# Full attention layers: scores issued in runs of three tiles (a key tile and a half), then the values of the run before, then side matmuls

## The chip, the cores and the metric
The kernel runs on one core of one Trainium2 chip. A core has TensorE (PE in the profile: matmuls; PEld: its weight loads), VectorE (DVE), ScalarE (ACT), GpSimd (POOL) and SyncE (SP), which issues most DMAs. The engines run by themselves and wait for each other through semaphores; each does its own instructions in the order in which they were written. The metric is the device time of one execution in microseconds (us), lower being better.

## The reference
Four attention layers stand one behind the other, on a sequence of 2048 rows of width 512 with 32 heads of 16. Layers 0 and 2 (weights A) see a window of 256 keys, layers 1 and 3 (weights B) all earlier and later keys:

```python
x = A_x
x = x + _A_ref(_layernorm(x, axis=-1), A_wqkv, A_wo)
x = x + _B_ref(_layernorm(x, axis=-1), B_wqkv, B_wo)
x = x + _A_ref(_layernorm(x, axis=-1), A_wqkv, A_wo)
x = x + _B_ref(_layernorm(x, axis=-1), B_wqkv, B_wo)

# _B_ref, after q, k, v = split(x @ wqkv):
scores = jnp.einsum("bhqd,bhkd->bhqk", q, k) * scale
p = _softmax(scores, axis=-1)
o = jnp.einsum("bhqk,bhkd->bhqd", p, v)
return (lambda x, *d: x.transpose(*d))(o, 0, 2, 1, 3).reshape(B, S, D) @ wo
```

## The kernel before
In a full layer the queries are cut into four chunks (`c`) of 512 and the heads into eight head groups (`qd`) of four; layer 3 also goes by quarters (`t`) of two groups each. For a chunk and a head group `attn_full` goes over sixteen key tiles (`j`) of 128 keys. So there are 32 head groups in each full layer, and 512 key tiles.

For a key tile, `exps` is called twice, for two heads each (`pr`). It makes a score tile, 128 keys x 2 heads x 512 queries, with two matmuls of 64 rows each (the two heads lie in different rows of the array and run side by side; q and k are split in high and low halves, and 64 rows hold these parts of a head). Then ScalarE takes the exponential of the whole tile, 128x1024, from PSUM into a tile `e` in SBUF. There are three score tiles in PSUM: two of the pool `ps_s` and one named `third`, taken in turn; a tile is used again when its exponential is done. There are six tiles `e` (`EB`).

The values (`pv`, L821) are four matmuls, one for each head, of 128 keys x 17 columns (16 of V and a column of ones that gives the denominator) by 512 queries in float32, into four strips of the accumulator `acc[0]`, where the sixteen key tiles are summed. They stand in a queue `pvq` and are issued by `flush(2)`: those of a key tile come after the scores of the second key tile behind it. When the last key tile of a head group is through, `epilogue` has VectorE read `acc[0]` (`ot`, L729), and the next group's values wait for that.

Behind the values of each key tile come side matmuls: the projections of q, k and v, and the output matmuls of other chunks and layers, which fill the second accumulator `acc[1]` in groups (L395, each of them in four strips of 32 columns). The class `Side` keeps them in a list. Its `step` is called once for each key tile, and `share` issues as many as a budget allows; the budget rises by the rest of the work over the rest of the steps, or by a least rate. `clock[0]` is the planner's own time, which says when a transfer or a read is expected to be done. TensorE's instructions come in just the order in which this code issues them (`manual_schedule`).

When a group of side matmuls of q or k is through, `project` has VectorE read `acc[1]` twice (L557 and L558: the rounded product, and what is left of it) and GpSimd square the rounded one (L563), for a bound on the scores.

The window layers use the same `exps`, `flush` and `Side`, with three tiles for a head group.

Of the kernel before, what the change touches and what calls it, by code (L numbers as in the profile page):

```python
# [9 lines left out]
F32 = mybir.dt.float32  # L10
# [19 lines left out]
R = 64  # L30
# [4 lines left out]
RUN = 4  # L35
L_MIN = 2.0 ** -90
# [153 lines left out]
def fast_path(ctx, tc, flag, a_x, a_wqkv, a_wo, b_wqkv, b_wo, out):  # L190
# [330 lines left out]
    def project(l, s, c, act, ht=None, first=False):  # L521
# [20 lines left out]
        for t in range(NHT) if ht is None else (ht,):  # L542
# [10 lines left out]
            with tc.high_priority(HEAD_START):  # L553
                if act:
                    nc.scalar.activation(sp[:, 0], ps, AF.Copy, scale=e)
                else:
                    nc.vector.tensor_scalar(sp[:, 0], ps, e, None, op0=ALU.mult)  # L557
                LAST["DVE"] = nc.vector.scalar_tensor_tensor(sp[:, 1], ps, e, sp[:, 0], op0=ALU.mult, op1=ALU.subtract).ins  # L558
            sq = vp.tile([P, QC], BF16, name=f"sq{n}_{t}", tag="sq", bufs=NHT)
            if act:  # L560
# [197 lines left out]

    def exps(name, kt, qt, pr, pieces):

        turn["s"] += 1
        ps = PH["third"] if PH["full"] and turn["s"] % 3 == 0 else ps_s.tile([P, 2, QC], F32, name=f"s{name}", tag="s")
# [6 lines left out]
        spent(0.27)  # L769
        e = pp.tile([P, 2, QC], F32, name=f"e{name}", tag="e", bufs=EB)  # L770
        LAST["ACT"] = nc.scalar.activation(e[:, :, w0:w1], ps[:, :, w0:w1], AF.Exp, scale=SCALE).ins  # L771
        return e

    def flush(n):
        while len(pvq) > n:
            spent(1.0)
# [35 lines left out]

    def attn_full(l, c, qd, kt, qt, a):
        for j in range(NT):
            es_ = []
            for pr in range(2):
                es_.append(exps(f"{l}_{c}_{qd}_{j}_{pr}", kt[j // 8], qt, pr, [(j % 8 * P, 0, QC, 0)]))

            def pv(j=j, es_=es_):
                for h in range(4):  # L820
                    nc.tensor.matmul(a[32 * h:32 * h + DH + 1, :], V[l, qd // 4, j // 8][:, j % 8, 4 * (qd % 4) + h, :],  # L821
                                     es_[h // 2][:, h % 2, :], start=(j == 0), stop=(j == NT - 1),
                                     skip_group_check=True)
            yield pv
# [106 lines left out]
    class Side:  # L931

        def __init__(self, steps, works=(), following=(), least=0.0):
            self.next, self.least = list(following), least
            self.q, self.steps, self.cost, self.spent, self.k = [], steps, 0.0, 0.0, 0
            self.budget = self.lag = 0.0
# [45 lines left out]
        def step(self):  # L982
            self.k += 1
# [16 lines left out]
        def share(self):  # L1000

            self.budget = min(self.budget + max((self.cost - self.spent) / max(self.steps - 3 - self.k, 1), self.least), 0.75)
            self.lag = max(self.lag - max(0.29, self.least), -0.3)
# [325 lines left out]
```

## Time and profile before
| | us |
|---|---|
| median of three runs | 2648.86 |
| lowest and highest run | 2648.67, 2651.83 |
| span of the profiled execution | 2650.4 |
| TensorE busy in it | 2579.3 (97%) |
| ScalarE busy | 2385.8 (90%) |
| VectorE busy | 844.9 (32%) |
| GpSimd busy | 582.9 (22%) |
| exponentials (L771), busy | 2248.1 in 2432 |
| values of the full layers (L821), busy | 1079.7 in 8192 |

No time of its own is kept for the profiled execution beside its span, which lies between the lowest and the highest run. The granted clock of TensorE is 0.996 of full speed in the mean. The full layers run from about 447 to 1400 us and from 1688 to 2635 us, the window layers before each of them.

How to read rows: a row of the order of time has its start, its length, the engine, the line, the operation, output<-input, and the shapes; x8 says that eight such instructions were merged, and the length is then that of them all. What stands in square brackets is the idle time ahead of it and what ended that. A float32 matmul of the values shows as two records, so x8 are the four heads of one key tile. In a row of windows stand the stretch, its length, and for each engine the busy time and the number of instructions.

### The profile page before, as it was taken

To read this page: it belongs to the slowest core of one execution; us is meant where nothing else is said; L and a number is where in the kernel's file an instruction comes from. 1 tells how busy PE (TensorE), PEld (TensorE's weight loads), DVE (VectorE), ACT (ScalarE), POOL (GpSimd) and SP (SyncE) were. 2 spreads that over 40 slices of the span, in tenths; PEclk is the share of its full clock that TensorE was granted. 3 is DMA by queue.
4 is the path that set the end of the run, shared out by engine and by line. 5 is a ranking of instruction groups with operands and counts; after the bars stand their busy time and mean duration, and the time that the engine had idled before them with its cause. 6 is when DMAs were issued, how large, how long until landed. Compare 5 with 4: busy or idle time off the path is not lost.

```text
span 2650.4 us, 63235 instructions
## 1 busy us (share of the span) xinstructions
PE 2579.3 (97%) x26201; PEld 771.5 (29%) x26201; DVE 844.9 (32%) x1947; ACT 2385.8 (90%) x2725; POOL 582.9 (22%) x1215
## 2 busy tenths in 40 slices
PE   8999899999999999999999999999999999999998
PEld 3333344322222222222223444422222222222221
DVE  5746653112332223112216666211111112222121
ACT  5777665999999999999997787699999999999997
POOL 1789760000000000000006788000000000000000
PEclk9999999999999999999999999999999999999999
DMA  6878766223342334222425655423222234435441
GB/s 206 195 229 274 209 197 184 59 97 122 101 108 91 96 114 121 75 76 86 136 69 167 206 159 152 147 77 95 83 77 69 85 106 143 147 113 168 131 134 50
DMA packets 293186, 341.34 MB, mean 129 GB/s; under 512 B 105929, under 2 KB 199593, under 8 KB 288281
## 3 DMA queue, kind: packets, MB, share of 16 engines
q1 hardware_dynamic: 284376, 310.17, 39.2%
q0 software_dynamic: 8512, 27.04, 3.8%
q8 instruction: 207, 3.39, 0.5%
q14 instruction: 91, 0.74, 0.1%
HBM read 226.49 MB, written 96.99 MB: 122 GB/s over the span
## 4 chain that ended last, share of the span: by engine, by line
PE 86%; ACT 6%; DVE 4%; issue 3%; DMA 1%; POOL 1%; SPq 0%; ACTq 0%; DVEq 0%
PE acc L821 34%; PE s L767 23%; PE acc L395 11%; PE b L398 7%; PE acc L855 6%; ACT e L771 5%; PE b L395 3%; PE bs L398 2%; DVE ot L729 1%; DMA x<-in_A_x_dram 0%; DVE xh L471 0%; POOL e L847 0%; PE acc L582 0%; DVE sp L558 0%; POOL e L844 0%
## 5 line engine op out<-in xcount | busy, mean ns | idle before, releaser
L771 ACT ACTIVATE e<-s 128x1024 f32<-128x1024 f32 (+2 forms) x2432 | 2248.1, 1091 | 106.8 <-PE s L767 95.7
L821 PE MATMUL acc<-e,vt 128*17 128x512 f32 x8192 | 1079.7, 599 | 4.3 <-DVE ot L729 3.3
L767 PE MATMUL s<-qt,kt 64*128 64x512 f16 (+3 forms) x5440 | 750.4, 354 | 23.3 <-ACT e L771 10.8
L767 PEld LDWEIGHTS <-kt 64*128 64x128 f16 x5440 | 190.3, 94 | 696.3 <-issue 680.0
L821 PEld LDWEIGHTS acc<-e,vt 128*17 128x17 f32 x8192 | 136.4, 95 | 396.2 <-issue 363.7
L847 POOL TENSOR_SCALAR_AFFINE_SELECT e<-e 128x256 f32<-128x256 f32 x512 | 233.4, 464 | 73.9 <-ACT e L771 72.9
L729 DVE STREAM_TRANSPOSE ot<-acc 128x512 f32<-128x512 f32 x128 | 91.4, 714 | 481.3 <-PE acc L821 375.5
L844 POOL TENSOR_SCALAR_AFFINE_SELECT e<-e 128x256 f32<-128x256 f32 x448 | 195.9, 444 | 42.5 <-ACT e L771 40.5
L855 PE MATMUL acc<-e,vt 128*17 128x384 f32 (+2 forms) x2816 | 197.9, 390 | 0.6 <-POOL e L844 0.5
L398 PE MATMUL b<-xc,w 128*128 128x512 f16 x520 | 125.4, 386 | 8.8 <-DMA xc<-xh 5.6
L671 DVE COPY vt<-acc 128x256 f32<-128x256 f32 (+1 forms) x48 | 23.6, 491 | 336.6 <-PE acc L395 336.6
L395 PE MATMUL acc<-wv,xc 128*32 128x256 f16 (+1 forms) x2304 | 120.6, 299 | 0.2 <-DVE km L598 0.2
L751 POOL TENSOR_TENSOR oh<-o,oh 128x512 f16<-128x512 f32 x19 | 22.1, 1162 | 433.0 <-DVE oh L750 429.7
L395 PEld LDWEIGHTS <-xc 128*32 128x32 f16 x2688 | 77.1, 97 | 137.7 <-issue 133.0
L676 POOL TENSOR_SCALAR vt<-vt 128x16 f32<-128x16 f32 (+1 forms) x48 | 11.1, 232 | 464.8 <-DVE vt L671 464.7
L395 PE MATMUL acc<-xc,w 128*32 128x512 f16 x1344 | 108.0, 379 | 0.0
L563 POOL TENSOR_TENSOR sq<-sp 128x512 bf16<-128x512 f16 x28 | 29.1, 1039 | 349.0 <-DVE sp L557 349.0
L395 PE MATMUL acc<-xc,w_h 128*32 128x512 f16 x1296 | 105.7, 379 | 0.0
L563 POOL TENSOR_TENSOR sq_h<-sp_h 128x512 bf16<-128x512 f16 x27 | 28.1, 1039 | 339.8 <-DVE sp_h L557 278.9
L712 DVE SCALAR_TENSOR_TENSOR x<-acc,x 128x512 f32<-128x512 f32 x60 | 41.4, 690 | 177.1 <-PE acc L395 164.7
L557 DVE TENSOR_SCALAR sp<-acc 128x512 f16<-128x512 f32 x28 | 19.4, 691 | 242.3 <-PE acc L395 242.3
L557 DVE TENSOR_SCALAR sp_h<-acc 128x512 f16<-128x512 f32 x27 | 18.5, 686 | 229.0 <-PE acc L395 229.0
(165 smaller groups left out, 1780.9 us busy)
## 6 DMA issues: line engine op xcount, KB each, us to landing
kt<-kf SPq DMA_DIRECT2D x126, 512.0 KB
xd<-x SPq DMA_DIRECT2D x96, 256.0 KB
qt<-qs SPq DMA_DIRECT2D x96, 256.0 KB
x<-xd SPq DMA_DIRECT2D x96, 256.0 KB
w<-wd SPq DMA_DIRECT2D x16, 1024.0 KB
qs<-sp SPq DMA_DIRECT2D x48, 256.0 KB
wv<-wd SPq DMA_DIRECT2D x20, 512.0 KB
x<-in_A_x_dram SPq DMA_DIRECT2D x32, 256.0 KB
```

The lines of the kernel that those rows point to most:

```text
L395: nc.tensor.matmul(ps[g:g + 32], a[:, g:g + 32], b, start=(i == 0), stop=(i == len(pairs) - 1), skip_group_check=True)
L398: nc.tensor.matmul(ps, a, b, start=(go and i == 0), stop=(i == len(pairs) - 1))
L557: nc.vector.tensor_scalar(sp[:, 0], ps, e, None, op0=ALU.mult)
L563: nc.gpsimd.tensor_tensor(sq, sp[:, 0], sp[:, 0], ALU.mult)
L712: nc.vector.scalar_tensor_tensor(xs[i], ps, 1.0 / (UP[2] * UP[3]), xs[i], op0=ALU.mult, op1=ALU.add)
L729: nc.vector.transpose(ot.rearrange("p b r -> p (b r)"), a)
L767: nc.tensor.matmul(ps[:, h, s0:s0 + wd_], kt[R * h:R * h + R, pr, kc:kc + P], qt[R * h:R * h + R, pr, qc:qc + wd_], start=True, stop=True)
L771: LAST["ACT"] = nc.scalar.activation(e[:, :, w0:w1], ps[:, :, w0:w1], AF.Exp, scale=SCALE).ins
L821: nc.tensor.matmul(a[32 * h:32 * h + DH + 1, :], V[l, qd // 4, j // 8][:, j % 8, 4 * (qd % 4) + h, :], es_[h // 2][:, h % 2, :], start=(j ...
L844: last = nc.gpsimd.affine_select(v, v, pattern=[[0, 2], [-1, P]], compare_op=ALU.is_gt, fill=0.0, base=0, channel_multiplier=1)
L847: last = nc.gpsimd.affine_select(v, v, pattern=[[0, 2], [1, P]], compare_op=ALU.is_ge, fill=0.0, base=0, channel_multiplier=-1)
L855: nc.tensor.matmul(a[32 * h:32 * h + DH + 1, q * P:(q + nb) * P], V[l, (4 * c + j) // 4][:, j % 4, 4 * qd + h, :], es_[h // 2][:, h % 2, s ...
```

## The change
A table `RUNS` cuts the sixteen key tiles of a head group into eleven runs: five times (tile j, first half of tile j+1) and (second half of tile j+1, tile j+2), and last tile 15 alone. "Half" is by queries: `exps_part` puts 256 queries of all four heads into one score tile (four matmuls of 256 columns), so that a key tile and a half are three score tiles and each exponential is still 128x1024. The matmuls of the values of a half are 256 wide and go to the half of the accumulator that they belong to. A run issues its three score tiles one behind the other, then `flush(1)` the values of the run before, and then the side matmuls.

`Side` counts in rooms now: the first run of a head group has room for four side matmuls, the next nine for two each, the last for none (22 for a head group); the budget may exceed a run's room by 1.2 matmuls. The planner's clock goes on by 0.903 for each score tile. In the full layers the square moves from GpSimd to VectorE and stands between its two reads of `acc[1]`.

On TensorE, in layer 1, chunk 2, head group 4, around key tile 7, there stood before (s are score tiles, s1_5721 is `third`, e exponentials, both with layer, chunk, head group, key tile and pair; acc0 and acc1 are the two accumulators; a wait on ScalarE reads Activation, one on VectorE DVE; left out are weight loads, the matmuls that complete a pair, and the other three strips of a side matmul):

```order
L767 MATMUL s1_2_4_7_0_13056<-qt1_2_4_12581,kt1_2_4_0_12583 128x512 [waits Activation_49]
...
L767 MATMUL s1_2_4_7_1_13061<-qt1_2_4_12581,kt1_2_4_0_12583 128x512 [waits Activation_49]
...
L821 MATMUL acc0_81<-e1_2_4_5_0_13020,vt1_1_0_5794 17x512 x2
L821 MATMUL acc0_81<-e1_2_4_5_1_13025,vt1_1_0_5794 17x512 x2
L395 MATMUL acc1_82<-xc2_1_12760,w2_1_1_12702 32x512
...
L767 MATMUL s1_5721<-qt1_2_4_12581,kt1_2_4_1_12585 128x512 [waits Activation_49]
...
L767 MATMUL s1_2_4_8_1_13078<-qt1_2_4_12581,kt1_2_4_1_12585 128x512 [waits Activation_49]
```

and now, with the pieces of a half named p0 and p1 (the rows left out are of the same kinds, and one side matmul of the following three is shown by its first strip):

```order
L786 MATMUL s1_2_4_6_0_13847<-qt1_2_4_13325,kt1_2_4_0_13327 128x512 [waits Activation_49]
...
L786 MATMUL s1_5721<-qt1_2_4_13325,kt1_2_4_0_13327 128x512 [waits Activation_49]
...
L834 MATMUL s1_2_4_7_p0_13856<-qt1_2_4_13325,kt1_2_4_0_13327 128x256 [waits Activation_49]
...
L858 MATMUL acc0_81<-e1_2_4_4_p1_13813,vt1_1_0_5823 17x256 x4
L858 MATMUL acc0_81<-e1_2_4_5_0_13817,vt1_1_0_5823 17x512 x2
L858 MATMUL acc0_81<-e1_2_4_5_1_13822,vt1_1_0_5823 17x512 x2
L399 MATMUL acc1_82<-xc2_1_13583,w2_1_1_13530 32x512 [waits DVE_49]
```

Two score tiles, each waiting for ScalarE, and one key tile of values have become three score tiles, each waiting, and one and a half key tiles of values; the buffers of the three are all that there are, in turn.

On TensorE at the end of layer 1, where the last score tile of head group 7 of chunk 3 is followed by the first of layer 2 (s2), there stood before:

```order
L767 MATMUL s1_3_7_15_1_16976<-qt1_3_7_16309,kt1_3_7_1_16313 128x512 [waits Activation_49]
...
L821 MATMUL acc0_81<-e1_3_7_13_0_16948,vt1_1_1_6659 17x512 x2
L821 MATMUL acc0_81<-e1_3_7_13_1_16952,vt1_1_1_6659 17x512 x2
L821 MATMUL acc0_81<-e1_3_7_14_0_16961,vt1_1_1_6659 17x512 x2
...
L821 MATMUL acc0_81<-e1_3_7_15_0_16974,vt1_1_1_6659 17x512 [waits Activation_49]
...
L821 MATMUL acc0_81<-e1_3_7_15_1_16979,vt1_1_1_6659 17x512 [waits Activation_49]
...
L767 MATMUL s2_0_0_0_0_17018<-qt2_0_0_17011,kt2_0_0_17010 128x384 [waits PE_49]
```

and now:

```order
L786 MATMUL s1_3_7_15_1_18206<-qt1_3_7_17442,kt1_3_7_1_17446 128x512 [waits Activation_49]
...
L858 MATMUL acc0_81<-e1_3_7_13_p1_18168,vt1_1_1_6768 17x256 x4
L858 MATMUL acc0_81<-e1_3_7_14_0_18173,vt1_1_1_6768 17x512 x2
...
L399 MATMUL acc1_82<-wv2_2_0_0_16848,xc2_2_16898 32x512 [waits DVE_49]
...
L858 MATMUL acc0_81<-e1_3_7_15_0_18204,vt1_1_1_6768 17x512 [waits Activation_49]
...
L858 MATMUL acc0_81<-e1_3_7_15_1_18209,vt1_1_1_6768 17x512 [waits Activation_49]
...
L786 MATMUL s2_0_0_0_0_18298<-qt2_0_0_18291,kt2_0_0_18290 128x384 [waits PE_49]
```

Twelve side matmuls (48 with their strips; `wv2_2` are the values' weights of layer 2, chunk 2) now stand between the values of tile 14 and of tile 15. Counted over the program, layer 1 has 748 side matmuls of 512 columns' worth (two of 256 counted as one) and layer 3 651, before and now.

The core of the diff:

```diff
+RUNS = [r for j in range(0, NT - 1, 3) for r in (((j, None), (j + 1, 0)), ((j + 1, 1), (j + 2, None)))] + [((NT - 1, None),)]
+ROOM = [4] + [2] * (len(RUNS) - 2) + [0]
+ROOMS = sum(ROOM)
+LATE = sum(ROOM[:8])
...
+                sq = vp.tile([P, QC], BF16, name=f"sq{n}_{t}", tag="sq", bufs=NHT)
+                if PH["full"]:
+                    nc.vector.tensor_tensor(sq, sp[:, 0], sp[:, 0], ALU.mult)
                 LAST["DVE"] = nc.vector.scalar_tensor_tensor(sp[:, 1], ps, e, sp[:, 0], op0=ALU.mult, op1=ALU.subtract).ins
-            sq = vp.tile([P, QC], BF16, name=f"sq{n}_{t}", tag="sq", bufs=NHT)
-            if act:
+            if PH["full"]:
+                pass
+            elif act:
...
+    def exponentials(name, ps, w0=0, w1=QC):
+
+        spent(0.23 if PH["full"] else 0.27)
+        e = pp.tile([P, 2, QC], F32, name=f"e{name}", tag="e", bufs=EB)
+        LAST["ACT"] = nc.scalar.activation(e[:, :, w0:w1], ps[:, :, w0:w1], AF.Exp, scale=SCALE).ins
+        return e
...
+        ps = score_tile(name)
-            spent(1.0)
+            spent(0.2 if PH["full"] else 1.0)
...
+    def exps_part(name, kt, qt, kc, half):
+
+        ps, w = score_tile(name), QC // 2
+        for pr in range(2):
+            for h in range(2):
+                nc.tensor.matmul(ps[:, h, pr * w:pr * w + w], kt[R * h:R * h + R, pr, kc:kc + P],
+                                 qt[R * h:R * h + R, pr, half * w:half * w + w], start=True, stop=True)
+        return exponentials(name, ps)
+
     def attn_full(l, c, qd, kt, qt, a):
-        for j in range(NT):
-            es_ = []
-            for pr in range(2):
-                es_.append(exps(f"{l}_{c}_{qd}_{j}_{pr}", kt[j // 8], qt, pr, [(j % 8 * P, 0, QC, 0)]))
-
-            def pv(j=j, es_=es_):
-                for h in range(4):
-                    nc.tensor.matmul(a[32 * h:32 * h + DH + 1, :], V[l, qd // 4, j // 8][:, j % 8, 4 * (qd % 4) + h, :],
-                                     es_[h // 2][:, h % 2, :], start=(j == 0), stop=(j == NT - 1),
-                                     skip_group_check=True)
+        for r, run_ in enumerate(RUNS):
+            PH["room"], PH["span"] = ROOM[r], 0.0
+            made = []
+            for j, half in run_:
+                n, k, kc = f"{l}_{c}_{qd}_{j}", kt[j // 8], j % 8 * P
+                if half is None:
+                    made.append((j, half, [exps(f"{n}_{pr}", k, qt, pr, [(kc, 0, QC, 0)]) for pr in range(2)]))
+                else:
+                    made.append((j, half, exps_part(f"{n}_p{half}", k, qt, kc, half)))
+                PH["span"] += 0.903 if half is not None else 1.806
+
+            def pv(made=made):
+                w = QC // 2
+                for j, half, e in made:
+                    for h in range(4):
+                        if half is None:
+                            to, fr = slice(0, QC), e[h // 2][:, h % 2, :]
+                        else:
+                            to, fr = slice(half * w, half * w + w), e[:, h % 2, h // 2 * w:h // 2 * w + w]
+                        nc.tensor.matmul(a[32 * h:32 * h + DH + 1, to], V[l, qd // 4, j // 8][:, j % 8, 4 * (qd % 4) + h, :],
+                                         fr, start=(j == 0), stop=(j == NT - 1), skip_group_check=True)
+                    spent(0.86 if half is None else 0.43)
             yield pv
...
-            self.k += 1
+            self.k += PH["room"] if PH["full"] else 1
...
-            self.budget = min(self.budget + max((self.cost - self.spent) / max(self.steps - 3 - self.k, 1), self.least), 0.75)
-            self.lag = max(self.lag - max(0.29, self.least), -0.3)
-            while self.q and clock[0] >= PH["free"] and self.budget >= MM / 2 and (self.lag < 0.25 or self.budget > 0.45):
+            room = PH["room"]
+            if not room:
+                return
+            self.budget = min(self.budget + room * max((self.cost - self.spent) / max(self.steps - 4 - self.k, 1), self.least), (room + 1.2) * MM)
+            while self.q and clock[0] >= PH["free"] and self.budget >= MM / 2:
                 c = self.one()
                 if c is None:
                     break
                 self.budget -= abs(c)
-                self.lag += abs(c)
...
-                    sd = sd or Side(NT * NQD // 2, works[0], works[1], 0.33)
+                    sd = sd or Side(ROOMS * NQD // 2, works[0], works[1], 0.24)
...
-                        clock[0] = max(clock[0], began + (2.4 if win else 1.8))
+                        clock[0] = max(clock[0], began + (2.4 if win else PH["span"]))
                         began = clock[0]
                         pvq.append([f])
-                        flush(2)
+                        flush(2 if win else 1)
```

The remaining lines replace `NT` by `ROOMS` and the least rates by the same per head group (0.33 x 16 by 0.24 x 22, 0.28 x 16 by 0.204 x 22), and the two points where a work has to be done by then.

22 lines of the change are left out of this document (10 added, 12 removed).

## The prediction
> **What bounds the kernel now.** I read the page first, then the two full layers alone (windows), then the order of time on TensorE and ScalarE inside them. The page says that TensorE is busy nearly all the time and ScalarE not much less, and that the chain that ended last runs 86% over TensorE:
>
> ```profile
> PE 2579.3 (97%) x26201; PEld 771.5 (29%) x26201; DVE 844.9 (32%) x1947; ACT 2385.8 (90%) x2725; POOL 582.9 (22%) x1215
> PE 86%; ACT 6%; DVE 4%; issue 3%; DMA 1%; POOL 1%; SPq 0%; ACTq 0%; DVEq 0%
> L767 PE MATMUL s<-qt,kt 64*128 64x512 f16 (+3 forms) x5440 | 750.4, 354 | 23.3 <-ACT e L771 10.8
> core 0: us, PE busy (x) PEld busy (x) DVE busy (x) ACT busy (x) POOL busy (x), PEclk, DMA share, GB/s
> 447.30:1399.60 952.30, 942.19 (x9408) 225.88 (x9405) 212.01 (x474) 946.93 (x1022) 53.13 (x71) 1.00 0.33 98
> 1688.30:2634.70 946.40, 935.88 (x9137) 234.76 (x9135) 174.73 (x383) 943.12 (x1024) 49.98 (x62) 1.00 0.35 105
> ```
>
> The last two rows are the full layers, 1 and 3, the only stages that the change orders anew. Both engines are 99% busy there, so the shares don't say which one sets the pace; the spacing does. Layer 1 does an exponential in 952.30/1022 = 0.932 us, layer 3 in 946.40/1024 = 0.924, and each layer has 1024, so they take 954 and 946 us, 1900 of the span of 2650.4.
>
> What ScalarE can do at most shows where there is little side work:
>
> ```profile
> 2449.07 1.99 ACT L771 ACTIVATE e<-s 128x1024 f32<-128x1024 f32 x2
> 2449.07 13.91 ACT L771 ACTIVATE e<-s 128x1024 f32<-128x1024 f32 x15
> ```
>
> Two exponentials end at 2451.06, fifteen at 2462.98: 11.92/13 = 0.917 us each. At that pace a layer takes 939 us. So ScalarE's floor for both layers is 1878, and only 22 us (15 and 7) lie between it and now. What lies between is TensorE's work, here in layer 1:
>
> ```profile
> 1041.77 0.40 PE L395 MATMUL acc<-xc,w 128*32 128x512 f16 x4
> 1042.10 0.61 PE L767 MATMUL s<-qt,kt 64*128 64x512 f16 x4
> 1042.64 1.05 PE L821 MATMUL acc<-e,vt 128*17 128x512 f32 x8
> 1043.51 0.61 PE L395 MATMUL acc<-xc,w 128*32 128x512 f16 x8
> 1044.06 0.61 PE L767 MATMUL s<-qt,kt 64*128 64x512 f16 x4
> ...
> 1052.13 1.05 PE L821 MATMUL acc<-e,vt 128*17 128x512 f32 x8
> 1053.11 0.60 PE L767 MATMUL s<-qt,kt 64*128 64x512 f16 x4
> ```
>
> Four score matmuls (two score tiles) take 0.54 us from their start to that of the values, the values 0.87, a side matmul 0.22 (0.33 from 1041.77 to 1042.10 with one, 0.55 from 1043.51 to 1044.06 with two), and 0.11 comes once before the next scores (without any side matmul they start 0.98 after the values). A key tile is 0.54 + 0.98 = 1.52 us plus 0.216 for each side matmul (0.55 less 0.33, in round figures), against 2 x 0.917 = 1.83 on ScalarE. TensorE is the later one with two side matmuls (1.95), ScalarE with one or none.
>
> **The change part by part.** *Fewer bursts.* Sixteen bursts of scores per head group become eleven. Of a burst's 0.54 the two pairs stream 0.43 (each is as wide as a side matmul, 0.216), so 0.11 is the switch to the values, and 0.11 is the switch back. That takes 5 x 0.22 = 1.1 us from TensorE per head group, 70 us over the 64 head groups, but the path can win only the 22 us down to ScalarE's floor. Splitting a key tile by queries should cost nothing by itself. The window layers have 256-wide pieces:
>
> ```profile
> 1435.08 0.63 PE L855 MATMUL acc<-e,vt 128*17 128x256 f32 x8
> 1435.52 1.91 PE L395 MATMUL b<-xc,w 128*32 128x512 f16 x32
> 1437.36 0.39 PE L767 MATMUL s<-qt,kt 64*128 64x256 f16 x4
> 1437.68 1.06 PE L855 MATMUL acc<-e,vt 128*17 128x384 f32 x16
> ```
>
> Two half-wide pairs of scores plus the switch take 0.32 (two full ones 0.54, so 0.11 for a half against 0.22), half-wide values 0.44 (half of 0.87). The pace of an exponential is unchanged, as its form is still 128x1024. Per run TensorE has 0.54 + 0.22 for three score tiles, 1.31 for one and a half tiles of values, 0.11 for the switch, and on average 748/351 = 2.1 side matmuls in layer 1 (counted in the new order) at 0.216: 2.64 us. ScalarE needs 2.75. By work alone TensorE is no longer the later one.
>
> *The wait that is added.* There are three score buffers, and a run fills all three back to back. Its third matmul pair can't start before the third exponential of the run before has ended, and everything on TensorE, values and side matmuls included, stands behind it. What such a wait costs is in the trace of before, where the second pair of a burst waits for the exponential that frees its buffer:
>
> ```profile
> 2450.59 0.92 PE L767 MATMUL s<-qt,kt 64*128 64x512 f16 x4
> 2451.11 0.39 PE L767 MATMUL s<-qt,kt 64*128 64x512 f16 x2
> 2451.44 1.05 PE L821 MATMUL acc<-e,vt 128*17 128x512 f32 x8
> 2449.98 2.00 ACT L771 ACTIVATE e<-s 128x1024 f32<-128x1024 f32 x2
> 2450.88 2.02 ACT L771 ACTIVATE e<-s 128x1024 f32<-128x1024 f32 x2
> 838.65 0.61 PE L767 MATMUL s<-qt,kt 64*128 64x512 f16 x4
> 839.14 1.02 ACT L771 ACTIVATE e<-s 128x1024 f32<-128x1024 f32 x1 [0.58 <-PE s L767]
> ```
>
> The burst at 2450.59 lasts 0.92 and not 0.61 us, because its second pair starts at 2451.11, 0.05 after an exponential ended (2451.06, above), and the values follow 0.33 later. The other two rows are a place where ScalarE had run dry: scores start at 838.65, their exponential at 839.14 and it ends at 840.16, 1.51 us after the scores' start.
>
> The page "TensorE: Matmul & The Clock Gate" of the Trainium skill (Part 3, The mechanism) states that matmuls are strictly first in, first out, without reordering. The trace agrees with that: the values at 2451.44 need nothing of the late pair and still start after it. By this rule the losses below stand; were it not so, the values would pass the late pair and the time would be the first rival's.
>
> So from the third pair of one run to the third pair of the run after next there is a round trip: 0.33 to the values; the values and side matmuls of that run; 0.11 to the next run's first scores; 1.51 to the end of their exponential; two exponentials more, 1.83; 0.05 to the matmul that waits for the last. That is 3.83 us plus values plus side matmuls, and ScalarE alone needs 6 x 0.917 = 5.50 for two runs. The work behind the waiting pair may thus be 1.67 us. Values take 1.31. One side matmul fits (1.52), two are 0.07 over, three 0.29 over, and nothing catches up, because ScalarE has no pace in hand. In the first run of a head group values are one key tile, 0.44 less, so four there count as two.
>
> The new order gives pairs of neighbouring runs by the longer of the two: layer 1 has 18 pairs that fit, 49 at 0.07, 2 at 0.18, 101 at 0.29 and 5 at 0.50, in sum 35 us; layer 3 has 50, 40, 1, 84 and 1, in sum 28. One run's loss covers its neighbour's, since the two round trips overlap; if it did not, the sums would be 51 and 42.
>
> *The end of layer 1.* Twelve side matmuls now stand between the values of tile 14 and those of tile 15 of the last head group: 12 x 0.216 = 2.6 us, with no scores behind them that would feed ScalarE. I count all of it.
>
> *The turn of a head group.* Before, the first values of a group waited for VectorE to read the accumulator:
>
> ```profile
> PEld acc L821 <- DVE ot L729: 16.9, 30, 1.5
> PEld acc L821 <- DVE ot L729: 10.4, 27, 0.7
> ```
>
> (layer 1, then layer 3). This is part of TensorE's lateness, thus of the 22 us, and isn't counted again. Now one run of side matmuls and three score tiles lie in between, more than the read takes.
>
> *The squares.* 55 of them move from GpSimd to VectorE, between the two reads of the side accumulator:
>
> ```profile
> L563 POOL TENSOR_TENSOR sq<-sp 128x512 bf16<-128x512 f16 x28 | 29.1, 1039 | 349.0 <-DVE sp L557 349.0
> L471 DVE TENSOR_TENSOR xh<-xn,xh 128x512 f16<-128x512 f32 x52 | 39.3, 756 | 1.6 <-ACT xh L466 0.4
> L750 DVE CAST oh<-o 128x512 f16<-128x512 f32 x52 | 25.1, 483 | 1.5
> L557 DVE TENSOR_SCALAR sp<-acc 128x512 f16<-128x512 f32 x28 | 19.4, 691 | 242.3 <-PE acc L395 242.3
> ```
>
> On VectorE a square isn't shown; the nearest rows are a cast of one operand (0.48) and an operation with two (0.76). The accumulator comes free that much later. What hides it are the scores and values of the run that follows, 0.76 + 1.31 = 2.07 us, against 0.69 for the first read, up to 0.76 and about 0.69 again for the second, 2.14. I take 0; the excess would be 55 x 0.07 = 4 us, and without the cover it is 55 x 0.76 = 42. GpSimd's 1.04 was off the path, so nothing is won.
>
> **The sum.** 2650.4 (the profiled span, which lies within the runs' 2648.67 to 2651.83) - 22 (down to ScalarE's floor) + 35 + 28 (round trips) + 2.6 = 2694. The median of the runs is 1.5 below that span; I predict 2693.
>
> **The rivals.** *ScalarE alone sets the pace*: the third pair finds its buffer free early enough, and TensorE's 2.64 stay hidden under 2.75. That gives 2650.4 - 22 + 2.6 = 2631, faster. For it speaks the work per run; against it the 0.05 and the 1.51 above. It needs a round trip about 0.3 us shorter than its rows say. The page "TensorEngine Tiling (Array Packing)" of the Trainium skill (Key Properties) says that a change of tiling mode drains the engine; the 0.22 per burst agree with that, and by this rule alone the kernel would come out here.
>
> *The wait and the gain cancel*: a round trip 0.2 us shorter (for instance if a pair's exponential ended 1.3 after it and not 1.51, where ScalarE has no earlier work queued). Two side matmuls then fit, three are 0.09 over: 185 x 0.09 + 6 x 0.3 = 18 us, 2650.4 - 22 + 18 + 2.6 = 2649, no change. Against it: the 1.51 is from just such a place.
>
> *Every long run pays for itself*: losses of neighbouring runs add up, 51 + 42: 2650.4 - 22 + 93 + 2.6 = 2724. It decides if the run that follows a late one can't use the time in which ScalarE stood; late reads of the side accumulator by VectorE would push the same way. That the change doesn't do what it says is excluded by the new order: eleven bursts per head group, as many exponentials.
>
> **How the numbers follow.** Forecast 0.63 (own range 2679 to 2707, from 0.05 us either way on 185 pairs with three side matmuls and 89 with two), ScalarE alone 0.14, cancelled 0.09, every run pays 0.14. The range of 2645 to 2720 leaves out the first rival and the upper half of the last. About 0.2% (5 us) is what a measurement of this kernel can tell from no change: faster 0.14 + 0.02, same 0.06 (the rest of the cancelled case is split), slower 0.78.
>
> **What would show it.** In the profile after: exponentials 0.94 to 0.96 us apart over each full layer; ScalarE idle before about every sixth exponential, ended by the scores; TensorE's scores waiting for ScalarE by tens of us, where the page has 10.8 in all; and the third pair of a run 0.05 after an exponential's end. Wrong would be the forecast if exponentials ran at 0.917 throughout, if the third pair never waited, or if the idle time of TensorE were ended by VectorE and not by ScalarE.

## The result, and the profile after

The changed kernel takes **2691.16 us** (median of four runs, 2687.18 to 2691.7) against 2649.64 (2648.67 to 2651.83) for the kernel before: a ratio of 1.0154, 95% interval 1.014 to 1.0169. The forecast was 2693. The profiled execution of the changed kernel, which the views show, is the shortest of its four runs (2687.18, span 2685.4): the span is 1.8 us shorter than the run's time, and 1.7 to 1.8 in every other run for which both are kept. By the same 1.8 us the profiled execution of the kernel before (span 2650.4) took 2652.2 us, a little over the longest of its runs, 2651.83. So the two spans differ by 35.0 us, and 6.5 of the 41.5 between the medians are not in the traces.

First the page: busy time by engine, the chain that ended last, the costliest groups of ScalarE and of the scores.

```profile
PE 2562.2 (95%) x30041; PEld 982.5 (37%) x30041; DVE 861.0 (32%) x2002; ACT 2401.9 (89%) x2725; POOL 525.8 (20%) x1160
PE 69%; ACT 20%; issue 5%; DVE 3%; DMA 1%; POOL 1%; ACTq 0%; SPq 0%; DVEq 0%
L776 ACT ACTIVATE e<-s 128x1024 f32<-128x1024 f32 (+2 forms) x1792 | 1703.1, 1033 | 112.2 <-PE s L786 95.9
L786 PE MATMUL s<-qt,kt 64*128 64x512 f16 (+3 forms) x4184 | 573.4, 344 | 50.4 <-ACT e_p L776 35.0
L834 PE MATMUL s_p<-qt,kt 64*128 64x256 f16 x1664 | 163.1, 272 | 22.4 <-ACT e L776 20.6
```

TensorE is busy 17 us less than before, though the program is 35 us longer, and part of the chain has moved from TensorE (86% before, 69% now) to ScalarE (6% before, 20% now). That fits a round trip between two engines: neither is busy all the time, and the chain passes from one to the other. The scores wait for ScalarE 35.0 + 20.6 us in these two groups alone, where the page before had 10.8.

The windows from the first exponential of a full layer to the last, both layers (stretch, its length, then busy time and instructions of each engine):

```profile
core 0: us, PE busy (x) PEld busy (x) DVE busy (x) ACT busy (x) POOL busy (x), PEclk, DMA share, GB/s
443.80:1416.70 972.90, 938.30 (x11310) 337.89 (x11311) 218.30 (x501) 956.36 (x1025) 24.14 (x42) 1.00 0.32 96
1704.80:2670.20 965.40, 925.84 (x11061) 333.11 (x11057) 182.35 (x410) 953.22 (x1024) 21.84 (x35) 1.00 0.34 104
```

In the kernel before the same windows read:

```profile
447.30:1402.40 955.10, 944.86 (x9430) 226.63 (x9426) 212.01 (x474) 949.74 (x1024) 53.13 (x71) 1.00 0.33 98
1688.30:2634.80 946.50, 935.98 (x9139) 234.79 (x9137) 174.73 (x383) 943.23 (x1024) 49.98 (x62) 1.00 0.35 105
```

By the starts of the 1024 exponentials of each layer the span divides like this:

| stretch of the span | before | after | difference |
|---|---|---|---|
| up to the first exponential of layer 1 | 447.3 | 443.8 | -3.5 |
| layer 1, first to last exponential | 954.1 | 971.8 | +17.7 |
| from there to the first of layer 3 | 287.0 | 289.2 | +2.2 |
| layer 3, first to last | 945.4 | 964.3 | +18.9 |
| from there to the end | 16.7 | 16.3 | -0.4 |
| span | 2650.4 | 2685.4 | +35.0 |

An exponential came every 0.932 and 0.924 us and comes every 0.950 and 0.943 now. The waits in the window of layer 1 (us in total, times, longest) name the two sides of it; VectorE's read at the turn of a head group (`ot`) is in the list no more:

```profile
PE s L786 <- ACT e_p L776: 17.2, 52, 0.5
PE s_p L834 <- ACT e L776: 10.2, 34, 0.7
PE s L834 <- ACT e L776: 3.5, 13, 0.4
ACT e L776 <- PE s L786: 7.4, 36, 0.6
ACT e_p L776 <- PE s_p L834: 4.1, 22, 0.2
ACT e_p L776 <- PE s L834: 1.8, 10, 0.2
```

And one round trip in the order of time, TensorE first, then ScalarE:

```profile
610.88 0.38 PE L786 MATMUL s<-qt,kt 64*128 64x512 f16 x2
611.65 0.39 PE L786 MATMUL s<-qt,kt 64*128 64x512 f16 x2 [0.39 <-ACT e_p L776]
611.97 1.05 PE L858 MATMUL acc<-e,vt 128*17 128x512 f32 x8
612.84 0.61 PE L858 MATMUL acc<-e_p,vt 128*17 128x256 f32 x8
613.27 0.83 PE L399 MATMUL acc<-xc,w 128*32 128x512 f16 x12
614.04 0.61 PE L786 MATMUL s<-qt,kt 64*128 64x512 f16 x4
...
614.53 1.94 ACT L776 ACTIVATE e<-s 128x1024 f32<-128x1024 f32 x2 [0.18 <-PE s L786]
```

The second pair (at 610.88) goes at once; the third stands until 611.65, because its buffer's exponential is late. Everything behind it is late by the same time: values at 611.97, three side matmuls at 613.27, the next run's first scores at 614.04. ScalarE has run dry by then and stands 0.18 us before its exponential at 614.53.

### The profile page after: what moved, and what is told of

Same layout as the page of the kernel before. It is cut to its first block, busy times and chain, and to the rows that moved or that the text cites. A ratio compares the mean times of both kernels' runs of the same rounds, so it can differ in the third digit from the quotient of the medians.

```text
span 2685.4 us, 70893 instructions
## 1 busy us (share of the span) xinstructions
PE 2562.2 (95%) x30041; PEld 982.5 (37%) x30041; DVE 861.0 (32%) x2002; ACT 2401.9 (89%) x2725; POOL 525.8 (20%) x1160
## 4 chain that ended last, share of the span: by engine, by line
PE 69%; ACT 20%; issue 5%; DVE 3%; DMA 1%; POOL 1%; ACTq 0%; SPq 0%; DVEq 0%
PE acc L858 24%; ACT e L776 15%; PE s L786 13%; PE acc L399 9%; PE b L402 7%; PE acc L892 5%; PE s_p L834 4%; ACT e_p L776 4%; PE b L399 3%; PE s L834 2%; PE bs L402 2%; POOL e L884 0%; POOL e L881 0%; DMA x<-in_A_x_dram 0%; DVE xh L475 0%
## 5 line engine op out<-in xcount | busy, mean ns | idle before, releaser
L776 ACT ACTIVATE e<-s 128x1024 f32<-128x1024 f32 (+2 forms) x1792 | 1703.1, 1033 | 112.2 <-PE s L786 95.9
L858 PE MATMUL acc<-e,vt 128*17 128x512 f32 x5632 | 740.3, 596 | 0.0
L786 PE MATMUL s<-qt,kt 64*128 64x512 f16 (+3 forms) x4184 | 573.4, 344 | 50.4 <-ACT e_p L776 35.0
L776 ACT ACTIVATE e_p<-s_p 128x1024 f32<-128x1024 f32 x425 | 439.4, 1052 | 9.0 <-PE s_p L834 7.6
L858 PE MATMUL acc<-e_p,vt 128*17 128x256 f32 x5120 | 397.4, 382 | 0.0
L786 PEld LDWEIGHTS <-kt 64*128 64x128 f16 x4184 | 188.8, 94 | 400.9 <-issue 377.3
L776 ACT ACTIVATE e_p<-s 128x1024 f32<-128x1024 f32 x215 | 226.7, 1054 | 4.1 <-PE s L834 3.5
L858 PEld LDWEIGHTS acc<-e_p,vt 128*17 128x17 f32 x5120 | 117.6, 96 | 278.3 <-issue 278.3
L834 PEld LDWEIGHTS <-kt 64*128 64x128 f16 x2512 | 103.1, 94 | 284.5 <-issue 244.2
L834 PE MATMUL s_p<-qt,kt 64*128 64x256 f16 x1664 | 163.1, 272 | 22.4 <-ACT e L776 20.6
L399 PE MATMUL acc<-wv,xc 128*32 128x256 f16 (+1 forms) x2304 | 103.8, 299 | 0.0
```

Source lines behind the costliest of these rows:

```text
L399: nc.tensor.matmul(ps[g:g + 32], a[:, g:g + 32], b, start=(i == 0), stop=(i == len(pairs) - 1), skip_group_check=True)
L786: nc.tensor.matmul(ps[:, h, s0:s0 + wd_], kt[R * h:R * h + R, pr, kc:kc + P], qt[R * h:R * h + R, pr, qc:qc + wd_], start=True, stop=True)
L834: nc.tensor.matmul(ps[:, h, pr * w:pr * w + w], kt[R * h:R * h + R, pr, kc:kc + P], qt[R * h:R * h + R, pr, half * w:half * w + w], start= ...
L858: nc.tensor.matmul(a[32 * h:32 * h + DH + 1, to], V[l, qd // 4, j // 8][:, j % 8, 4 * (qd % 4) + h, :], fr, start=(j == 0), stop=(j == NT ...
```

## The experiments

The theory is the forecast's: a third pair waits for the third exponential of the run before, and the values and side matmuls behind it close a round trip over two runs. The rivals: TensorE's amount of work (half tiles, weight loads, switches), VectorE's squares, and the score buffers by themselves, whatever stands behind.

**At most two side matmuls behind a run.**

```diff
-ROOM = [4] + [2] * (len(RUNS) - 2) + [0]
+ROOM = [4] + [2] * (len(RUNS) - 1)
-... (room + 1.2) * MM)
+... (room + 0.45) * MM)
```

> The changed kernel, but at most two side matmuls behind the values of a run (four behind the first run of a head group, as before; the last run of a group takes two as well). Now 119 runs in layer 1 and 116 in layer 3 have three behind one and a half key tiles of values; in this order none has, while the number of side matmuls is the same. What doesn't fit is done in lumps: 40 and not 12 behind the last scores of layer 1, and some 24 more than fit at three places of layer 3. The round trip (as in the prediction) says: no pair of runs loses 0.29 us, most lose 0.07, which is 351/2 x 0.07 = 12 us in layer 1 where it was 35, and about 9 in layer 3 where it was 28: 42 us won. The lumps cost (28 + 24) x 0.216 = 11 us. So 31 us under the changed kernel's 2691: about 2660, and exponentials 0.93 us apart in layer 1. Rival, TensorE's amount of work (half tiles, weight loads, switches) makes the change slow: the amount is the same, so 2691, or up to 2702 with the lumps. Rival, VectorE's squares are late: 2691 too.

Measured: 2696.03 us (2694.1 to 2703.83), 1.0181 of the kernel before (1.0157 to 1.0205). The total is 36 us above the expectation and no better than the changed kernel. The cycles inside a head group are as expected: six exponentials take 5.57 us. But at 27 turns of a head group in layer 1 ScalarE loses 0.55 us at once, 15 of the 27.9 us that this layer lies above ScalarE's floor; the other 13 are near the expected 12. Layer 3 lies 32.8 us above the floor where 14 were expected (9 and 24 side matmuls in lumps); 22 of them are lost at turns, 14 in five stops of over 0.9 us. The order of time at such a turn, TensorE and then ScalarE:

```profile
653.78 0.61 PE L786 MATMUL s<-qt,kt 64*128 64x512 f16 x4
654.32 0.63 PE L858 MATMUL acc<-e_p,vt 128*17 128x256 f32 x8
654.76 1.04 PE L858 MATMUL acc<-e,vt 128*17 128x512 f32 x8
655.62 0.61 PE L399 MATMUL acc<-xc,w 128*32 128x512 f16 x8
656.17 0.61 PE L786 MATMUL s<-qt,kt 64*128 64x512 f16 x4
656.66 1.02 ACT L776 ACTIVATE e<-s 128x1024 f32<-128x1024 f32 x1 [0.44 <-PE s L786]
```

The last run of a group has two score tiles (653.78), but behind it stand the values of a long run and the two side matmuls that this edit put there: 2.4 us of TensorE against 1.83 of ScalarE. The edit had brought a loss of its own, and the lumps cost more than expected, as the next run shows.

**The same, with nothing behind the last run of a group** (its room is 0, as in the change; the limit of 0.45 stays):

> At most two side matmuls behind a run, four behind the first of a head group and none behind the last, which has two score tiles only. It differs from the run with two behind the last one too in that table alone. There the cycles came at 5.57 us as expected, but 28 head groups of layer 1 lost another 0.55 us at their turn, where two runs of work stood against five exponentials. Reading of it: 0.05 + 2 x (0.33 + 1.31 + 0.43 + 0.11) - ... by its rows 5.07 us against 5 x 0.917 = 4.59; without the two side matmuls 4.64, 0.05 over. So the 0.55 should go: layer 1 from its first to its last exponential 939 + 13 = 952 us, within 3, where the changed kernel has 971.8 and the run with two behind the last 966.0. Lumps: 97 side matmuls and not 12 behind the last scores of layer 1, 18 us; layer 3 has lumps of 14.5, 14.5, 8 and 6. So the whole gains little: about 2685 (2676 to 2694). Rival, the turn of a head group costs 0.55 us for another cause (values wait for VectorE's read of the accumulator, or four side matmuls behind the first run): layer 1 stays at 964 to 967.

Measured: 2748.85 us (2746.36 to 2751.02), 1.0359 (1.0334 to 1.0383). Layer 1, the point of the run, took 952.5 us from its first to its last exponential; 952 was expected:

```profile
444.40:1397.00 952.60, 931.72 (x10956) 324.94 (x10956) 213.18 (x484) 950.92 (x1025) 23.12 (x39) 1.00 0.31 94
```

No turn of the kind seen above is left. The total missed by 64 us, and nearly all of that lies in the lumps: what doesn't fit into the runs now stands where no scores cover it, and costs far more there than the 0.216 us for each that was expected:

```profile
1401.81 2.77 PE L399 MATMUL acc<-xc,w 128*32 128x512 f16 x48 [1.85 <-DVE sp L565]
1406.43 2.77 PE L399 MATMUL acc<-xc,w 128*32 128x512 f16 x48 [1.85 <-DVE sp L565]
1422.13 2.77 PE L399 MATMUL acc<-wv,xc 128*32 128x512 f16 x48 [0.79 <-DVE vt L679]
```

Twelve side matmuls (48 rows) take 2.6 us and then TensorE stands 1.85 or 0.79 us until VectorE has read their accumulator. In layer 3 fifteen stops of over 0.35 us sum to 64 of the 75.9 us that it lies above ScalarE's floor. By itself the pace of layer 1 in these two runs doesn't tell the round trip from TensorE's work, since 28 and 85 side matmuls have left the layer (6 and 18 us). What tells them apart are the cycles (below): the layer's total is no proof.

**Up to five behind every second run, none between.**

```diff
-ROOM = [4] + [2] * (len(RUNS) - 2) + [0]
+ROOM = [4] + [0, 5] * 4 + [0, 0]
```

(with the limit of 0.45 as above)

> The changed kernel, with the same side matmuls dealt out unevenly: up to five behind every second run of a head group and none behind the runs between. The round trip from a third pair to that of the run after next holds the side matmuls of one run only, so five behind one run cost 3.83 + 1.31 + 5 x 0.216 - 5.50 = 0.72 us in two runs, though TensorE's work over the two is no more than with two and three (5 x 0.216 and 2 x 2.19, which is 5.46 us). In the order layer 1 has 73 such runs, 18 with three and 16 with two: 59 us against 35 in the changed kernel; layer 3 has 47 with five and 55 with three: 50 against 28. Lumps that fit nowhere: 123 more side matmuls behind the last scores of layer 1, some 60 more in layer 3: 40 us. Together 2691 + 24 + 22 + 40 = 2777; where five stand behind a run, six exponentials take 6.22 us. Rival, TensorE's amount of work: only the lumps, 2731, and six exponentials take 5.5 to 5.6 us there.

Measured: 2896.73 us (2894.74 to 2898.02), 1.0929 (1.0911 to 1.0947). Above the expected 2777, for the reason just seen: the stops of over 0.9 us in the full layers sum to 102 us, and 346 us lie between the two layers, where it was 289. Without those stops layer 1 lies 57.7 us above ScalarE's floor (59 expected) and layer 3 50.5 (50 expected). A cycle:

```profile
704.25 0.40 PE L834 MATMUL s_p<-qt,kt 64*128 64x256 f16 x4 [0.48 <-ACT e L776]
704.57 0.63 PE L858 MATMUL acc<-e_p,vt 128*17 128x256 f32 x8
705.02 1.04 PE L858 MATMUL acc<-e,vt 128*17 128x512 f32 x8
705.88 1.26 PE L399 MATMUL acc<-xc,w 128*32 128x512 f16 x20
707.07 0.39 PE L834 MATMUL s_p<-qt,kt 64*128 64x256 f16 x4
707.57 1.02 ACT L776 ACTIVATE e_p<-s_p 128x1024 f32<-128x1024 f32 x1 [0.62 <-PE s_p L834]
```

The five side matmuls (705.88) need nothing of the late pair and stand behind it all the same, as the page "TensorE: Matmul & The Clock Gate" of the Trainium skill (Part 3, The mechanism) has it with its first in, first out.

From rows like these, over the cycles of the traces of the changed kernel and of this uneven one: the time from the start of a run's third pair to that of the run after next, in which ScalarE makes six exponentials, by the side matmuls behind the two runs (medians; both runs with one and a half key tiles of values). The forecast's terms are 3.83 + 1.31 + 0.216 for each side matmul behind the first run, or ScalarE's 5.50 if that is more.

| kernel, layer | side matmuls behind first and second run | cycles | us | by the forecast's terms |
|---|---|---|---|---|
| changed, 1 | 0 and 0 | 17 | 5.50 | 5.50 (ScalarE) |
| uneven, 1 | 1 and 0 | 9 | 5.50 | 5.50 (ScalarE) |
| uneven, 1 | 2 and 0 | 9 | 5.57 | 5.57 |
| changed, 1 | 2 and 2 | 49 | 5.57 | 5.57 |
| uneven, 3 | 3 and 0 | 48 | 5.79 | 5.79 |
| changed, 1 | 3 and 2 | 39 | 5.78 | 5.79 |
| changed, 1 | 3 and 3 | 37 | 5.79 | 5.79 |
| uneven, 1 | 5 and 0 | 53 | 6.22 | 6.22 |

Three and none take longer (5.79) than two and two (5.57), though TensorE has less to do, and three and three no longer than three and none. In these cycles only what stands behind the first run counts. That rules out TensorE's amount of work.

The table leaves out other kinds of cycles, most of them with more behind the second run than behind the first, and there the time can lie above the first run's terms. None and five in the uneven layer 1 take 6.16 us (72 cycles): the stop that the five of the run ahead have caused falls into that time. None and one take 5.71 there (13), two and three 5.66 in the changed layer 1 (29), two and one 5.71 in its layer 3 (14); the cause of these was not followed up.

**Side matmuls half as wide**, in the kernel before and in the changed one. These two kernels leave out half of each product's columns, so their results are not the reference's; they only serve to time the rest:

```diff
-nc.tensor.matmul(ps[g:g + 32], a[:, g:g + 32], b, ...
+nc.tensor.matmul(ps[g:g + 32, :wide(b)], a[:, g:g + 32], b[:, :wide(b)], ...
```

> The kernel before, with each side matmul of the full layers half as wide (half of its product's columns is left out, and the flag that sends the program to its slower general path is held at the value that keeps it off). Only to be compared with the changed kernel cut in the same way. TensorE needs 1.52 + 0.109 for each side matmul per key tile, at most 1.85 with three, against ScalarE's 1.83: ScalarE's floor, 2650 - 22 = 2628, by each theory.

> The changed kernel, with each side matmul of the full layers half as wide (half of its product's columns is left out, and the same flag is held). Round trip with three of them: 3.83 + 1.31 + 0.33 = 5.47 us, inside ScalarE's 5.50. So nothing is lost any more: within 5 us of the kernel before cut in the same way, 2625 to 2633. Rival, half tiles, their weight loads, the squares or the new order cost the time by themselves: still some 40 us slower than the kernel before cut in the same way. Rival, every run's wait (the score buffers by themselves, whatever stands behind): the same 40.

Measured: 2627.95 us (2626.62 to 2629.95) and 2627.5 (2626.05 to 2629.27), ratios to the uncut kernel before of 0.9912 (0.9895 to 0.9928) and 0.9913 (0.9896 to 0.9929). The 41 us between the two orders are gone. The windows of the full layers, first of the kernel before with narrow side matmuls, then of the changed one:

```profile
448.60:1389.10 940.50, 923.41 (x9428) 261.92 (x9425) 212.22 (x474) 938.81 (x1025) 53.07 (x71) 1.00 0.32 99
1675.50:2612.60 937.10, 920.13 (x9133) 255.29 (x9134) 174.86 (x383) 937.10 (x1024) 49.94 (x62) 1.00 0.35 106
```

```profile
444.60:1384.60 940.00, 878.96 (x11322) 328.03 (x11323) 218.19 (x501) 939.81 (x1025) 23.89 (x42) 1.00 0.33 99
1671.20:2609.90 938.70, 874.46 (x11061) 322.75 (x11057) 182.21 (x410) 938.62 (x1024) 21.76 (x35) 1.00 0.35 107
```

ScalarE is busy from end to end in all four, and the cycles of the changed order take 5.50 us whatever stands behind the pair. The same waits on the same buffers are there, with half tiles, their weight loads and the squares; they cost nothing once the work behind the third pair is short enough. By itself this run would fit TensorE's amount of work too, since that shrinks with the side matmuls; the cycles above tell the two apart. A gain shows as well: TensorE is busy 90 us less in the changed order's two windows (1753 against 1844; short waits that count as busy may be part of either), only ScalarE has no use for it.

**The runs undone**, one key tile each, all else as in the change:

```diff
-RUNS = [r for j in range(0, NT - 1, 3) for r in ...
+RUNS = [((j, None),) for j in range(NT)]
+ROOM = [2, 1, 1, 2, 1, 1, 2, 1, 1, 2, 1, 2, 1, 2, 1, 1]
```

> The changed kernel with its runs alone undone: 16 runs of one key tile each (two score tiles, values of the run before the last one's scores as in the change, lag of one), with all else of the change: squares on VectorE, the new room table and the new pace of side matmuls, 22 rooms per head group. Round trip: with two score tiles in a run the third buffer is always free in time, so it goes like the kernel before, 2650 within 5. Rival, the squares, the rates or the lag of one cause the loss: 2691 or near it.

Measured: 2733.25 us (2731.3 to 2736.6), 1.032 (1.0302 to 1.0337): 83 us over the expectation and slower than the change. No wait of TensorE on the page says why. Its values, beside those of the kernel before (groups by line: busy us, mean ns of one, idle before):

```profile
L858 PE MATMUL acc<-e,vt 128*17 128x512 f32 x8192 | 1204.3, 598 | 3.7 <-DVE ot L737 3.2
```

```profile
L821 PE MATMUL acc<-e,vt 128*17 128x512 f32 x8192 | 1079.7, 599 | 4.3 <-DVE ot L729 3.3
```

As many matmuls of the same length, but 125 us more busy time. In the order of time a key tile's values last longer than the 1.05 us of the rows before. The first two rows are such values; the third is the later part of the second row, and the fourth the exponentials beside it:

```profile
1045.05 1.25 PE L858 MATMUL acc<-e,vt 128*17 128x512 f32 x8
1046.77 1.36 PE L858 MATMUL acc<-e,vt 128*17 128x512 f32 x8
1047.09 0.72 PE L858 MATMUL acc<-e,vt 128*17 128x512 f32 x4
1045.09 1.95 ACT L776 ACTIVATE e<-s 128x1024 f32<-128x1024 f32 x2
```

The four heads of a key tile no longer start together but in two groups: the second (1047.09) waits for the tile's second exponential, which with the values only one short run behind has not ended; it ends at 1047.04, 0.05 us before. While the first group is in flight that wait counts as busy. So the expectation failed on the lag: "the third buffer is always free in time" was true, but the values had become the late ones. The next run puts the lag back:

```diff
-                        flush(2 if win else 1)
+                        flush(2)
```

> The kernel with runs of one key tile (the run before this one in the study), but with the values two tiles behind the scores, as in the kernel before; squares, room table and pace of side matmuls stay those of the change. With values one tile behind, the traces showed TensorE's values for the second half of a key tile waiting for an exponential that had not ended (four matmuls that run side by side split in two and two), and 85 us lost. Round trip: that wait belongs to one-tile runs at a lag of one and not to squares or rates; with the lag of two back the kernel goes like the one before, 2650 to 2658 (62 tiles of layer 1 have three side matmuls where 22 had). Rival, squares, room table or pace of the side matmuls cost the time: 2691 or above.

Measured: 2657.27 us (2655.79 to 2664.2), 1.003 (1.0018 to 1.0041), inside the expected 2650 to 2658. With runs of one key tile, squares on VectorE, the room table and the new pace together cost about these 8 us.

**The side matmuls between the second and the third score tile.**

```diff
-            made = []
+            made, left = [], 3 if len(run_) > 1 else 9
...
+                    for pr in range(2):
+                        left -= 1
+                        if not left:
+                            yield None
+                        made[-1][2].append(exps(f"{n}_{pr}", k, qt, pr, [(kc, 0, QC, 0)]))
                 else:
+                    left -= 1
+                    if not left:
+                        yield None
                     made.append((j, half, exps_part(f"{n}_p{half}", k, qt, kc, half)))
```

(where `None` comes, the caller issues the side matmuls; the lines for that are left out)

> The changed kernel, but the side matmuls of a run are issued between its second and its third score tile, not behind the values. That takes them out of the round trip (3.83 + 1.31 = 5.14 us against ScalarE's 5.50 for two runs) and adds a switch from scores and back, 0.22 us, in the 288 runs of layer 1 and 266 of layer 3 that have side matmuls. Round trip: TensorE's work sets the pace in layer 1, per head group 32 x 0.216 + 16 x 0.87 + 22.7 x 0.216 + 20 x 0.22 = 30.1 us against 29.3 on ScalarE, thus 26 us over ScalarE's floor for 32 head groups; layer 3 about level with ScalarE, some 6 over it. That is 2650 - 22 + 26 + 6 + 2.6 = 2663, 28 under the changed kernel. Rival, TensorE's work and switches are what the change costs: 554 switches more x 0.22 = 122 us, about 2810. Rival, VectorE's squares: 2691.

Measured: 2705.87 us (2701.3 to 2715.5), 1.0219 (1.019 to 1.0248): 43 us above the expectation and far from the rival's 2810. The order of time and the window of layer 1:

```profile
1189.84 0.38 PE L786 MATMUL s<-qt,kt 64*128 64x512 f16 x2
1190.15 0.61 PE L399 MATMUL acc<-xc,w 128*32 128x512 f16 x8
1190.70 0.39 PE L786 MATMUL s<-qt,kt 64*128 64x512 f16 x2
...
1192.43 0.61 PE L786 MATMUL s<-qt,kt 64*128 64x512 f16 x4
...
1195.26 0.39 PE L834 MATMUL s_p<-qt,kt 64*128 64x256 f16 x4
```

```profile
447.30:1427.30 980.00, 967.81 (x11296) 279.04 (x11297) 219.90 (x501) 961.14 (x1025) 23.93 (x42) 1.00 0.32 95
```

The third pair finds its buffer free, and TensorE is busy 968 of 980 us: it is the bound now. A run with two side matmuls takes 2.83 us (1192.43 to 1195.26), with three 3.04 (from 1186.57 to 1189.61 in the same trace), against ScalarE's 2.75. The expectation set the mean of a head group against ScalarE (26 and 6 us over the floor in layers 1 and 3); if every run had to pay its own excess, summed over the runs of this trace, it would be some 55 and 50; measured are 41.8 and 32.2. Runs with few side matmuls make up only a part of what the others lose. So this run shows that the wait can be removed, and that the place between the scores is too dear.

**The squares back on GpSimd.**

```diff
-                sq = vp.tile(...)
-                if PH["full"]:
-                    nc.vector.tensor_tensor(sq, sp[:, 0], sp[:, 0], ALU.mult)
```

> The changed kernel with the squares back on GpSimd, all else as in the change. Round trip: within 4 us of the changed kernel, 2687 to 2693. Rival, the accumulator of the side matmuls comes free too late because of the squares: faster by up to 55 x 0.76 = 42 us, with TensorE waiting for VectorE less than in the changed kernel.

Measured: 2688.9 us (2687.48 to 2693.45), 1.0154 (1.0135 to 1.0172), the changed kernel's ratio. The squares are out of it.

## Why the prediction was right, point by point

- *ScalarE's floor of 0.917 us, 22 us to win.* Right: with the side matmuls narrowed, the layers take 939.4 and 937.0 us in the one order and 938.8 and 937.6 in the other, from first to last exponential; the forecast had 939 for each, and the runs came 22 us under the kernel before.
- *70 us less work for TensorE.* Not measured cleanly: 90 by the busy time of the narrow pair, only 17 in the two layers of the changed kernel itself (1864 against 1881). That part of a wait counts as busy (last section) is the likely reason.
- *The round trip of 3.83 us plus work, over two runs.* Right in each size of the table: 5.50 with none or one side matmul, 5.57 with two, 5.78 to 5.79 with three, 6.22 with five. The third pair starts 0.05 us after an exponential's end in nearly all of some 480 late cases in the changed kernel's trace. The other signs named are there as well: exponentials 0.950 and 0.943 us apart, scores waiting for ScalarE by tens of us, and an exponential over 0.05 us later than ScalarE's pace allows 190 and 168 times in a layer, about every sixth.
- *One run's loss covers its neighbour's.* Right: three and three take no longer than three and none. The rival in which every long run pays, 93 us above the floor, falls with this; measured are 60.
- *35 and 28 us.* The layers lie 33.7 and 26.2 us above ScalarE's floor, where they lay 16.0 and 7.3 before: +17.7 and +18.9 where the forecast's terms make +20 and +21.
- *The end of layer 1, 2.6 us.* Between the layers the trace shows +2.2.
- *The squares at nothing.* Right, and the square itself was below the range given for it (0.48 to 0.76 us):

```profile
L564 DVE TENSOR_TENSOR sq<-sp 128x512 bf16<-128x512 f16 x28 | 11.8, 423 | 0.7
```

  With 0.42 us the two reads and the square stay under the 2.07 us of cover.
- *The turn of a head group inside the 22.* The waits for VectorE's read of `acc[0]` (`ot`) are gone in the full layers, and no run spoke against counting it once. ScalarE still loses some 0.12 us at 20 turns of layer 1 (2.4 us there in all, 1.4 in layer 3); the forecast has no term for that.
- *ScalarE alone sets the pace*, and *wait and gain cancel*, would have needed a shorter round trip; at 5.79 us it is as long as its rows said. Narrow side matmuls give the first of them: with the work behind the pair shortened, the order runs at ScalarE's pace. By fewer switches alone the change would have been faster; what they save on TensorE is worth nothing here, as ScalarE and the round trip set the pace. The page "TensorEngine Tiling (Array Packing)" (Key Properties) of the Trainium skill says that a change of tiling mode drains the engine.
- *What it had not:* layer 1 begins 3.5 us earlier in the changed kernel's trace, though TensorE's order is the same up to there. Over the profiles of this study its first exponential comes between 441.4 and 448.7 us. This wasn't followed up, and its cause stays open; without it the span would have been 5 us below the sum.
- *The number, 2693 against 2691.* That it came so near is in part luck. The sum added 43.6 us to a span; the traces show 35.0, the medians 41.5. In the traces the two layers' terms are 4.4 us too large together, the earlier start of layer 1 takes 3.5 more, and the two ends 0.8; but the execution whose span the sum starts from was longer than the four runs of the kernel before, and the profiled one of the changed kernel was its shortest.

No complete kernel of this study is faster than the kernel before. At up to three side matmuls behind a run the change loses more than the 22 us that it can win, and where they are held to two, the rest stands uncovered and costs more.

## What to carry to other kernels

When a burst of work grows to use all buffers between two engines, its last piece waits for the consumer, and all that is queued behind it on an in-order engine joins a round trip. Add that trip up (wait, work behind it, first new result, the consumer's remaining work) and set it against the consumer's own time for the same span, since busy shares and work per step, which said "faster" here, don't show it. Spread the filler work by the slack of that trip, not by its mean, and price what then fits nowhere with its reader's time.

## What the runs showed of the hardware that was not expected

- **A wait can hide in busy time.** With the values one short run behind, 125 us more "busy" stood on the same 8192 matmuls of the same mean length (1204.3 against 1079.7), and no line of TensorE's waits named them; only the rows' lengths, 1.25 and 1.36 for 1.05 us, did. In the changed kernel a short wait of the scores shows no idle time either. Here are two rows of its order of time, each with two pairs of the same kind:

```profile
1011.14 0.59 PE L786 MATMUL s<-qt,kt 64*128 64x512 f16 x4
...
1016.71 0.74 PE L786 MATMUL s<-qt,kt 64*128 64x512 f16 x4
```

  The second lasts 0.15 us longer because its second pair starts that much later, and no idle time is written to it, since the pair before is shown for 0.39. The page "Perfetto Trace Analysis" of the Trainium skill (Tensor Engine Instruction) says that the end of a TensorE row is computed and not observed; these rows agree with that.
- **An uncovered group of side matmuls costs its reader as well:** twelve take 2.6 us and then 1.85 us (or 0.79) until VectorE has read them, so up to 4.4 and not 2.6. Three expectations went wrong or partly wrong on that one term.
- **The square of 16-bit operands took 0.42 us on VectorE**, less than the cast of as many elements (0.48) that was its lower bound.
